# A retention-and-gated-FFN kernel: one load of v issued later on GpSimd, and a gate block put ahead of one transposition

## The chip, the cores and the metric

One Trainium2 chip, one core of it. The metric is the device time of one execution in microseconds (us), median of the runs shown.

## The reference, cut to what matters

```python
def _attn_ref(q, k, v):                     # q, k, v: (4, 8, 768, 64)
    gamma = 1.0 - 2.0 ** (-5.0 - np.arange(H))
    for t in range(S):
        state = gamma * state + einsum('bhd,bhe->bhde', k[:, :, t], v[:, :, t])
        y[:, :, t] = scale * einsum('bhd,bhde->bhe', q[:, :, t], state)

def _moe_ref(x, w_gate, w_val, w_out):      # x: (3072, 512), d_ff = 1536
    gate = 1.0 / (1.0 + np.exp(-(x @ w_gate)))
    val = x @ w_val
    return gate * val @ w_out
```

The output of the first, with heads side by side, is the x of the second. Inputs and output are float32.

## The kernel before, in words

The sequence of 768 is cut into six tiles of 128 positions; the four batch entries go through together, two at a time. A **pair** P is tile P // 2 with batch entries 0 and 1 (P even) or 2 and 3 (P odd), so there are 12 pairs; a pair has two **chunks**, its two batch entries. For each pair k and q are brought to the transposed layout qkT: by TensorE transposes for pairs 0 to 3 (`transpose`, L200, and the eviction `turned_out`, L210), by DMA transposes from SP for pairs 4 to 11 (`xbar`, L219). Then come the scores (`scores`, L238), the masks that take them out of PSUM on VectorE (`mask`, L243), the part of y that comes from the carried state (`inter`, matmuls of zbd and qkT), the part within the tile (`intra`, L258), y's way into xT (`y_out`, L271 or L273), and the state update (`state`, L280, and what follows it). A matmul that `mm` issues is one of 128x128 at L305, or two of 64 columns at L309, by a flag.

For each tile of 512 tokens the FFN then multiplies xT by the gate and value weights (`up`, `up_half`; from tile 1's later part on by a scheme of seven half-size products, which needs sums of weight blocks), applies the sigmoid on ScalarE, the product on VectorE or GpSimd, and the down projection. The sums of weight blocks are `weight_sums` (L456, into wt and scr) and `halves_sums` (L361, into ws, wg, wv); hidden ones are `hidden_sums` (L474).

Nothing is scheduled by a planner when the kernel is built: the order of the work is a written list, `ORDER`, of six strings. Each word is a step with two letters and a number; a capital first letter makes `mm` issue whole matmuls, a small one halves, and + and - say which tile's FFN is meant. Each engine executes its own instructions in this order. The steps that the change and the prediction speak of:

- `in4`, `ia4`, `yo4`: `inter`, `intra`, `y_out` of pair 2, chunk 0; with 5 of pair 2, chunk 1. `mk8` and `mk9` are the two masks of pair 2, chunk 0; `mk10` and `mk11` those of chunk 1.
- `tp6`, `te6`: the TensorE transposes of pair 3's k and their eviction on ScalarE; `tp7`, `te7` those of pair 3's q.
- `vm10`, `vm11`, `mu10`, `mu11`: value blocks of tile 0 on TensorE and their products on VectorE. `ag2`, `ag6`: gate blocks of tile 1 (256 columns, two blocks of hidden units each).
- `sc6`, `sc8`, `sc10`: scores of chunk 0 of pairs 3, 4 and 5. `sm5`, `sm6`: state update of pairs 5 and 6. `xk4`, `xq4`, `xk5`, `xq5`: DMA transposes of pairs 4 and 5.
- `wp..`, `wc..`: weight sums on GpSimd and their copies out on ScalarE. `hg6`: a hidden sum of tile 0 on GpSimd (L474).

Loads of k, q and v and of the weights go out on GpSimd's queue (`load`, L96; L116; L120), in program order and mixed with GpSimd's arithmetic. All loads up to pair 5 stand ahead of the first step of `ORDER`. Buffers rotate by the digits in `PLACES`; ff are the seven PSUM banks.

Of the kernel before, what the change touches and what calls it, by code (L numbers as in the profile page):

```python
# [17 lines left out]
def kernel(  # L18
# [38 lines left out]
        "gs": "01234501234503215034203502345102354130524301453201540321453034035412031524",  # L57
        "maskd": "01",
        "ff": (
            "012345601230465102346523105246310542631405314056321602341562034163412045632516523560132601562306"  # L60
            "251062562015020324512065630653102651604250142343624015405400652016203541034046326504510416035253"
            "245132541351025162405034123406520512341234160532120605410531324"
        ),
        "qkT": "010231230123",
        "kt": "0101100101",
        "st": "012345670123456702134675120346752104637563245710",
        "xT": "010101",
        "hT": "010101",
        "scr": "010101101001101010010101010101",
# [12 lines left out]
    def held_in(P, n):  # L82
        held = {"k": kn, "q": qn, "v": vn}[n]
        t, j = divmod(P, 2)
        if (n, t) not in lands:
            lands[n, t] = place(ld, [C, 4 * H, D], BF16, tag=n, name=n + "n")
        for i in range(2):
            held[2 * t + i] = lands[n, t][:, i * 2 * H:(i + 1) * 2 * H, :]
        return held[P]

    def load(P, *what, pairs=1):
        t, j = divmod(P, 2)
        for n in what:
            held_in(P, n)
            x = {"k": k, "q": q, "v": v}[n]
            nc.gpsimd.dma_start(out=lands[n, t][:, j * 2 * H:(j + pairs) * 2 * H, :],  # L96
                                in_=x[2 * j:2 * (j + pairs), :, t * C:(t + 1) * C, :].rearrange("b h s d -> s (b h) d"))
# [85 lines left out]
    qkT, kt, sc, st, y, zz, za, xT = {}, {}, {}, {}, {}, {}, {}, {}  # L183
# [377 lines left out]
    def hold(P):  # L561
        nc.gpsimd.tensor_copy(kept[:, :2], qkT[P][:, :, 1, NP - 1, C - 1])

    def hold_for_sums(t):
        nc.gpsimd.tensor_copy(kept[:, 2:3], hs[t][:, 2, NFF // 2 - 1, :1])
# [53 lines left out]
    for s in range(4):  # L619
        load_out(s)  # L620
    load(4, "k", "q", "v")
    load(5, "k", "q", "v")

    STEPS = {
        "gm": lambda t, n: up(t, n, 0),
# [38 lines left out]
        "lk": lambda t, P: load(P, "k", pairs=2),  # L664
        "lq": lambda t, P: load(P, "q", pairs=2),
        "lv": lambda t, P: load(P, "v", pairs=2),
        "ho": lambda t, P: hold(P),
        "hi": lambda t, n: hold_for_sums(t),
        "xk": lambda t, P: xbar(P, 0),
# [128 lines left out]
```

## Time and profile before

| | us |
|---|---|
| time, median of 3 runs | 224.1 (215.31 to 226.42) |
| time of the profiled execution | 215.9 |
| its span, first to last instruction | 214.2 |
| TensorE busy | 204.6 (96%) |
| VectorE busy | 189.2 (88%) |
| ScalarE busy | 147.5 (69%) |
| GpSimd busy | 139.5 (65%) |

The shares are averages over stages with different limits. In the rows, PE is TensorE, PEld its weight loads, DVE VectorE, ACT ScalarE, POOL GpSimd, SP the sync engine; a row of the timeline has the start in us, the duration in us, then engine, line, operation, output and input, the number of instructions merged, and in brackets the idle time of the engine ahead of it with what ended it.

### The profile page before, as it was taken

What the parts mean: (1) busy time and instruction counts of PE and PEld (TensorE: products, weight loads), DVE (VectorE), ACT (ScalarE), POOL (GpSimd) and SP (SyncE); (2) the same over time, 40 slices, a digit from 0 to 9 for tenths busy, and PEclk for the clock granted to TensorE, in tenths of its full rate; (3) what the DMA queues carried; (4) which work ended last, traced back from release to release, by engine and by line L of the source; (5) the groups of instructions that cost most, each with busy time, mean ns of one, the idle gap of its engine ahead of it and who ended that gap; (6) DMA issues with size and microseconds to landing.
All of it is one profiled execution on the core that took longest, in us unless ns stands there. A gap on an engine that the chain in (4) does not pass through costs nothing.

```text
span 214.2 us, 7187 instructions
## 1 busy us (share of the span) xinstructions
PE 204.6 (96%) x2938; PEld 177.3 (83%) x2938; DVE 189.2 (88%) x406; ACT 147.5 (69%) x396; POOL 139.5 (65%) x145
## 2 busy tenths in 40 slices
PE   6778999999999999999999999999999999999994
PEld 6555555778888998899988889998899988888883
DVE  6587979989999999979999899999999999968971
ACT  6384466543994389786869798787768969577731
POOL 8977784679999946699764279875618537024500
PEclk9999999999999999999999999999999999999999
DMA  9999999999995999969995129998121000023305
GB/s 125 143 170 194 195 173 165 183 199 159 159 132 33 98 156 143 204 126 157 170 227 115 49 99 163 159 105 127 49 101 52 3 0 3 0 50 70 75 25 183
DMA packets 103922, 25.38 MB, mean 118 GB/s; under 512 B 93904, under 2 KB 101072, under 8 KB 103888
## 3 DMA queue, kind: packets, MB, share of 16 engines
q0 software_dynamic: 81104, 13.90, 84.6%
q1 hardware_dynamic: 22640, 10.88, 28.6%
q8 instruction: 23, 0.38, 0.7%
q10 hardware_dynamic: 144, 0.13, 0.2%
q14 instruction: 11, 0.09, 0.1%
HBM read 28.31 MB, written 6.29 MB: 162 GB/s over the span
## 4 chain that ended last, share of the span: by engine, by line
PE 76%; DMA 14%; POOL 4%; DVE 3%; issue 1%; ACT 0%; ACTq 0%; DVEq 0%; POOLq 0%
PE ff L305 41%; PE ff L309 29%; DMA qn<-in_q_dram 6%; DMA wg<-in_moe_w_gate_dram 4%; DMA vn<-in_v_dram 4%; PE ff L238 2%; PE ff L258 2%; DVE scr L414 1%; POOL kn L96 1%; PE z L280 1%; DVE gs L435 1%; DVE xT L273 1%; POOL vn L96 1%; POOL qn L96 1%; POOL kn L104 1%
## 5 line engine op out<-in xcount | busy, mean ns | idle before, releaser
L420 POOL TENSOR_TENSOR hT<-gs,scr 128x512 bf16<-128x512 f32 x17 | 22.1, 1302 | 21.4 <-ACT gs L440 9.0
L430 ACT COPY gs<-ff 128x256 f32<-128x256 f32 x72 | 25.6, 377 | 11.1 <-PE ff L305 5.7
L409 ACT COPY scr<-ff 128x256 f32<-128x256 f32 x72 | 25.2, 375 | 6.5 <-PE ff L309 3.6
L414 DVE TENSOR_TENSOR scr<-scr,ff 128x512 f32<-128x512 f32 (+1 forms) x48 | 25.6, 547 | 3.5 <-ACT scr L409 1.3
L435 DVE TENSOR_TENSOR gs<-gs,ff 128x512 f32<-128x512 f32 (+1 forms) x48 | 25.8, 548 | 3.2 <-PE ff L305 2.0
L510 ACT COPY ob<-ff 128x256 f32<-128x256 f32 x48 | 17.7, 375 | 15.2 <-PE ff L305 8.9
L243 DVE TENSOR_TENSOR st<-ff,maskd 128x512 bf16<-128x512 f32 x40 | 25.7, 682 | 0.9 <-PE ff L238 0.9
L440 ACT ACTIVATE gs<-gs 128x512 f32<-128x512 f32 (+1 forms) x48 | 24.7, 530 | 2.3 <-DVE gs L435 2.2
L309 PE MATMUL ff<-xT,wg 128*64 128x256 bf16 (+1 forms) x268 | 24.2, 308 | 0.0
L309 PEld LDWEIGHTS <-wg 128*64 128x64 bf16 x356 | 19.4, 110 | 4.1 <-issue 0.4
L423 POOL TENSOR_TENSOR hT<-gs,scr 128x256 bf16<-128x256 f32 x16 | 11.9, 747 | 15.9 <-ACT gs L440 12.0
L309 PE MATMUL ff<-xT,wv 128*64 128x256 bf16 (+1 forms) x220 | 21.5, 311 | 0.0
L305 PEld LDWEIGHTS <-hT 128*128 128x128 bf16 x198 | 19.2, 98 | 2.7 <-issue 0.2
L305 PE MATMUL ff<-wo,hT 128*128 128x256 bf16 x156 | 21.0, 273 | 0.0
L309 PEld LDWEIGHTS <-wv 128*64 128x64 bf16 x312 | 17.2, 110 | 4.2 <-issue 0.3
L305 PEld LDWEIGHTS <-wv 128*128 128x128 bf16 x184 | 17.7, 98 | 2.4
L305 PEld LDWEIGHTS <-wg 128*128 128x128 bf16 x162 | 15.7, 98 | 3.8 <-issue 1.1
L309 PE MATMUL ff<-xs,ws 128*64 128x256 bf16 x208 | 18.7, 273 | 0.0
L305 PE MATMUL ff<-xT,wv 128*128 128x256 bf16 (+1 forms) x134 | 18.5, 276 | 0.0
L231 ACT ACTIVATE kt<-kn,tabk 128x128 bf16<-128x128 bf16 x48 | 18.3, 405 | 0.1
L309 PEld LDWEIGHTS <-ws 128*64 128x64 bf16 x308 | 17.2, 110 | 0.3
L305 PE MATMUL ff<-xT,wg 128*128 128x256 bf16 x110 | 15.4, 272 | 1.6 <-ACT xT L271 1.6
(118 smaller groups left out, 526.8 us busy)
## 6 DMA issues: line engine op xcount, KB each, us to landing
out_dram<-ob SPq DMA_DIRECT2D x18, 256.0 KB, 3.3
vn<-in_v_dram POOLq DMA_DIRECT2D x6, 256.0 KB, 12.4
wo<-in_moe_w_out_dram POOLq DMA_DIRECT2D x4, 384.0 KB, 14.2
kn<-in_k_dram POOLq DMA_DIRECT2D x3, 512.0 KB, 7.8
qn<-in_q_dram POOLq DMA_DIRECT2D x3, 512.0 KB, 10.0
vn<-in_v_dram POOLq DMA_DIRECT2D x3, 512.0 KB, 11.6
out_dram<-ob SPq DMA_DIRECT2D x11, 128.0 KB, 2.2
kn<-in_k_dram POOLq DMA_DIRECT2D x5, 256.0 KB, 13.4
```

What stands on the lines that cost most here:

```text
L231: nc.scalar.activation(to[:, :, h, :], x[:, :, h, :], AX.Copy, scale=tabk[:, 0, h:h + 1])
L243: nc.vector.tensor_tensor(st[P, c, i], sc[P, c][i], (mask0 if P < 2 else maskd)[:, i], op=ALU.mult)
L305: nc.tensor.matmul(o, left, right, skip_group_check=True, **kw)
L309: nc.tensor.matmul(o[half], left[:, half], right, skip_group_check=True, **kw)
L409: nc.scalar.copy(vals[t, g][:, {1: 0, 5: 2, 3: 1}[n]], m[False][:, 256:] if n == 1 else m[True][:, :256])
L414: nc.vector.tensor_tensor(o, o, x, op=ALU.add)
L420: eng.tensor_tensor(h[:, 2 * g], s, vals[t, g][:, 0:2].rearrange("p two n -> p (two n)"), op=ALU.mult)
L423: eng.tensor_tensor(h[:, 2 * g + 1, 256:], s[:, 256:], vals[t, g][:, 2], op=ALU.mult)
L430: nc.scalar.copy(o, pairs[t, g, 0][x][:, :256] if x else pairs[t, g, 0][x][:, 256:])
L435: nc.vector.tensor_tensor(o, o, pairs[t, g, 0][False][:, cols], op=ALU.add)
L440: nc.scalar.activation(o, x, AX.Sigmoid)
L510: nc.scalar.copy(o, fast[t, i][x][:, :256] if x else fast[t, i][x][:, 256:])
```

## The change

The load of pair 5's v leaves the block of loads and becomes a step, `lw5`, behind `hg6`. In the second string of `ORDER` pair 2's chunk 0 moves ahead: its masks go in front of tile 0's last products, `in4` and `ia4` in front of `vm11`, and `in4` is issued in halves. The gate block `ag2` goes between `tp6` and `tp7`. Three more words move by a few places: `dc11`, `dc15` and `hs7` of tile 0, and in the third string `sm6`, which now stands behind `gs57`. The digits of `PLACES` for the banks and for st follow the new order.

```diff
-    load(5, "k", "q", "v")
+    load(5, "k", "q")
...
+        "lw": lambda t, P: load(P, "v"),
...
-        "zo0- wp1 gm7- ... sg10- mu6- mu8- mk10- mk8-  "
-        "mk11- wp8 vm10- mu10- wp2 in5 ia5 vm11- IN4 mk9- ia4 yo5 tp6 yo4 aw13 sg11- te6 mu11- tp7 te7 dd5 dd15  "
-        "ag2 ag6 kt24 xk5- as2 sc6 ...
+        "zo0- wp1 gm7- ... sg10- mu6- mu8- mk10- mk11-  "
+        "mk8- mk9- wp8 vm10- wp2 in5 in4 ia5 ia4 yo5 yo4 vm11- mu10- tp6 aw13 sg11- te6 mu11- ag2 tp7 te7 dd5  "
+        "dd15 ag6 kt24 xk5- as2 sc6 ...
...
-        ... zo6 hg6- BV0 AV0 ...
+        ... zo6 hg6- lw5 BV0 AV0 ...
...
-        ... ia15 gp44 ga56 gs56 va56 vf46 vf56 sm6 vp47 va47 in14 gp57 ga57 gs57 vp57
+        ... ia15 gp44 ga56 gs56 va56 vf46 vf56 vp47 va47 in14 gp57 ga57 gs57 sm6 vp57
```

On GpSimd, at the end of the block of loads and then 14 rows later (kn, qn, vn are the landing tiles of k, q and v; ws, wt, scr and wg belong to the weight sums, hT to `hg6`):

```order
 L96 DMA qn<-in_q_dram 128x16x64
-L96 DMA vn<-in_v_dram 128x16x64
 L361 TENSOR_TENSOR ws<-wv 128x256
 L456 TENSOR_TENSOR wt<-wo 128x512
...
 L361 TENSOR_TENSOR wg<-wg 128x2x128
 L474 TENSOR_TENSOR hT<-hT 128x2x256
+L96 DMA vn<-in_v_dram 128x16x64
 L456 TENSOR_TENSOR wt<-wo,scr 128x512
 L456 TENSOR_TENSOR scr<-wo 128x512
```

The load of v has moved past 14 instructions of arithmetic on GpSimd.

On VectorE, where pair 2's masks (st), its y (xT) and tile 0's last products (hT) stand:

```order
-L243 TENSOR_TENSOR st<-ff,maskd 128x512 x3
-L332 TENSOR_TENSOR hT<-gs,ff 128x512
-L243 TENSOR_TENSOR st<-ff,maskd 128x512
-L273 TENSOR_TENSOR xT<-ff,taby_138 128x4x128 x2
-L332 TENSOR_TENSOR hT<-gs,ff 128x512
+L243 TENSOR_TENSOR st<-ff,maskd 128x512 x4
+L273 TENSOR_TENSOR xT<-ff,taby_138 128x4x128 x2
+L332 TENSOR_TENSOR hT<-gs,ff 128x512 x2
```

The same eight instructions: the fourth mask and the two of y now stand ahead of both products.

More of the change, by code (lines that the diff above doesn't have):

```diff
@@ L59 @@
         "ff": (
-            "012345601230465102346523105246310542631405314056321602341562034163412045632516523560132601562306"
-            "251062562015020324512065630653102651604250142343624015405400652016203541034046326504510416035253"
-            "245132541351025162405034123406520512341234160532120605410531324"
+            "012345601230465102346523105246310542631405314056321632045631205430541256301643610634201432461036"
+            "142361461324313015421364603640231642635143251050615324534533641326130452305356016435423526304140"
+            "154201452042314261534305210536413421052105263401213634523402015"
         ),
@@ L65 @@
         "kt": "0101100101",
-        "st": "012345670123456702134675120346752104637563245710",
+        "st": "012345670123456701234675210346751204637563145720",
         "xT": "010101",
```

14 rows, old and new, of the table ORDER are left out of this document.

## The prediction

> **What bounds the kernel now.** I read the page's shares first, then the busy time by stages, then the chain that ended last, and then the timelines of the four engines around the moved steps. The profiled execution took 215.9 us, 1.7 us more than its span of 214.2; all sums below are made against that execution. It stands near the lowest of the three runs shown (215.31), 8.2 us under their median of 224.1, and no profile of a run at 224 exists.
>
> ```profile
> 41.00:62.00 21.00, 20.98 (x282) 18.39 (x283) 19.87 (x35) 14.42 (x31) 19.04 (x19) 1.00 1.89 170
> 62.00:77.00 15.00, 15.00 (x276) 13.73 (x276) 14.54 (x28) 8.02 (x20) 14.82 (x15) 1.00 1.25 86
> 77.00:111.00 34.00, 33.86 (x601) 31.36 (x596) 32.24 (x76) 26.84 (x81) 24.40 (x26) 1.00 1.69 174
> 111.00:175.00 64.00, 63.98 (x1019) 59.14 (x1017) 60.50 (x130) 52.00 (x150) 39.50 (x37) 1.00 0.72 87
> ```
>
> These rows of the busy time by stages (stage, its length, then busy time of PE, PEld, DVE, ACT, POOL, the granted clock, DMA share, GB/s) say that from 41 us on TensorE has no hole worth the name, at a granted clock of 1.00. So a step that only changes places behind 41 us is worth nothing unless it opens a hole, and a gain can come only from the stretch where TensorE still waits for a load. That stretch is in the chain that ended last:
>
> ```profile
> 27.54 13.44 DMA qn<-in_q_dram
> 41.02 0.64 PE ff L200 x16
> ```
>
> Pair 3's q, issued at 27.54 us, lands at 40.98, and `tp7` starts on it at once. From there the chain is TensorE nearly to the end.
>
> **The early part: the new order around `tp7`.** TensorE and the two engines that feed it, before:
>
> ```profile
> 37.94 0.39 PE L309 MATMUL ff<-qkT,zbd 128*64 128x128 bf16 x8
> 38.16 0.52 PE L258 MATMUL ff<-st,vn 128*64 128x128 bf16 x8
> 38.49 1.05 PE L309 MATMUL ff<-xT,wv 128*64 128x512 bf16 x8
> 39.48 0.40 PE L305 MATMUL ff<-qkT,zbd 128*128 128x128 bf16 x4
> 39.81 0.41 PE L258 MATMUL ff<-st,vn 128*64 128x128 bf16 x8
> 40.05 0.61 PE L200 MATMUL ff<-ident,kn 128*64 128x128 bf16 x16
> 41.02 0.64 PE L200 MATMUL ff<-ident,qn 128*64 128x128 bf16 x16 [0.36 <-DMA qn<-in_q_dram]
> 41.49 1.91 PE L309 MATMUL ff<-xT,wg 128*64 128x256 bf16 x32
> 43.34 0.62 PE L238 MATMUL ff<-qkT 64*128 64x128 bf16 x16
> ```
>
> ```profile
> 36.36 1.89 DVE L243 TENSOR_TENSOR st<-ff,maskd 128x512 bf16<-128x512 f32 x3
> 38.22 0.69 DVE L332 TENSOR_TENSOR hT<-gs,ff 128x512 bf16<-128x512 f32 x1
> 38.82 0.68 DVE L243 TENSOR_TENSOR st<-ff,maskd 128x512 bf16<-128x512 f32 x1
> ```
>
> ```profile
> 40.71 2.01 ACT L210 COPY qkT<-ff 128x1024 bf16<-128x1024 bf16 x2 [2.34 <-PE ff L200]
> ```
>
> Each row is start, duration, engine, line, operation and tiles. They are, from the top, `in5`, `ia5`, `vm11`, `in4` (whole), `ia4`, `tp6`, `tp7`, `ag2` with `ag6`, `sc6`; three masks, `mu10`, the fourth mask; `te6` with `te7`. What one costs is the distance of starts: a halved `in` 0.22 us, the whole one 0.33, an `ia` 0.22 to 0.24, `vm11` 0.87, `tp6` 0.44, `tp7` 0.47, a gate block 0.925 (half of 43.34 - 41.49). The one stall that is named is 0.36 us at `tp7`; the whole `in4` also starts about 0.13 us after `vm11` has had its 0.87.
>
> Now the new order from 37.94. `in5`, `in4` and `ia5` end at 37.94 + 3 x 0.22 = 38.60. `ia4` needs the fourth mask, which has lost `vm11` as its cover: three masks end at 36.36 + 1.89 = 38.25, the fourth starts at 38.22 where `mu10` stood and ends at 38.90; with 0.05 to start, `ia4` runs at 38.95, after **a new stall of 0.35 us**, and ends at about 39.15. `vm11` to 40.02, `tp6` to 40.46. `ag2` needs both parts of y, which VectorE now takes straight after the masks at 0.60 each from 38.85: ready at about 40.15, so `ag2` goes at 40.46 and ends at 41.39. Pair 3's q has been there since 40.98, so `tp7` does not wait: 41.39 to 41.86. `ag6` to 42.78. But `sc6` needs `te7`. A transposition's records last to 0.64 us behind its start and ScalarE follows 0.04 later: `te7` goes at 41.39 + 0.68 = 42.07 and takes half of 2.01, to 43.07. So `sc6` starts at about **43.10 instead of 43.34, a gain of 0.24 us**, with TensorE idle for the 0.32 us ahead of it. Of the 0.36 us of the load, most goes to the fourth mask and to `te7`: what is late next is ScalarE's eviction, since only one gate block now lies behind `tp7` where two did.
>
> Bounds: if neither the mask nor `te7` held TensorE up, the gain would be 0.36 + 0.13 + 0.11 (the halved `in4`) = 0.60 us; if `te7` comes as late as before, nothing. I take the worked 0.24.
>
> **The load of v: GpSimd's side.** The moved load is 1.14 us of GpSimd, with 0.59 us of waiting ahead of it.
>
> ```profile
> 44.68 1.14 POOL L96 DMA_DIRECT2D qn<-in_q_dram  x1 [0.89 <-DMA wo<-in_moe_w_out_dram]
> 46.41 1.14 POOL L96 DMA_DIRECT2D vn<-in_v_dram  x1 [0.59 <-DMA wo<-in_moe_w_out_dram]
> ...
> 54.98 1.16 POOL L456 TENSOR_TENSOR scr<-wo 128x512 f32<-128x512 bf16 x1 [0.25 <-ACT wo L460]
> ...
> 62.06 1.21 POOL L456 TENSOR_TENSOR wt<-wo,scr 128x512 bf16<-128x512 bf16 x1
> ...
> 79.96 1.15 POOL L474 TENSOR_TENSOR hs<-hT,hs 128x512 bf16<-128x512 bf16 x1 [3.10 <-PE ff L309]
> ```
>
> The sums begin at 45.82 instead of 47.56, 1.74 us earlier. That head start dies at 54.98, where a sum waits until ScalarE has copied scr out (L460), and ScalarE gets there in its own order behind the gates of TensorE; it comes only the 0.24 us earlier. So `hg6`, the instruction ahead of 62.06, ends at about 61.8, the load of v is issued from 61.8 to 63.0, and what stands behind it on GpSimd is **0.9 us later than before**. Behind it are a sum that ScalarE copies out at 66.35, pair 6's loads, and xs; the 3.10 us of waiting ahead of 79.96 takes the delay up. ScalarE's copy goes from 66.35 to 67.2, but its next gate waited 0.94 us for TensorE, which covers that:
>
> ```profile
> 66.35 0.62 ACT L460 CAST wt<-scr 128x512 bf16<-128x512 f32 x1 [1.28 <-POOL scr L456]
> 67.91 0.60 ACT L345 ACTIVATE gs<-ff 128x512 f32<-128x512 f32 x1 [0.94 <-PE ff L305]
> ```
>
> I cost it at nothing; with that cover gone it would be up to 0.9 us.
>
> **The load of v: the queue's side.** v is first read by `sm5`, the state update of pair 5.
>
> ```profile
> 64.29 0.62 PE L238 MATMUL ff<-qkT 64*128 64x128 bf16 x16
> 69.02 0.62 PE L238 MATMUL ff<-qkT 64*128 64x128 bf16 x16
> 69.58 0.44 PE L280 MATMUL z<-vn,kt 128*64 128x64 bf16 x16
> ```
>
> The rows are `sc8`, `sc10` and `sm5`, which would come at 69.34. How long 256 KB take from 61.8 no row shows: before, issued at 46.41, the load queued behind everything else for the 17.5 us of the first row below. The page's rows of DMA issues (KB each, median us to landing) bound it. Below: 4.9 us, what 128 KB took at the start. Above: 12.4, the median of v's 256 KB loads. Nearest are the 512 KB loads of k, which go out when the queue has run empty: 7.8. I take 6.4, between 4.9 and 7.8: landing at 68.2, **1.1 us ahead of `sm5`**, so nothing is paid. At 7.8 it is 69.6 and 0.3 us are lost.
>
> ```profile
> DMA to landing us min/median/max: 17.5/17.5/17.5
> ```
>
> ```profile
> vn<-in_v_dram POOLq DMA_DIRECT2D x6, 256.0 KB, 12.4
> kn<-in_k_dram POOLq DMA_DIRECT2D x3, 512.0 KB, 7.8
> kn<-in_k_dram POOLq DMA_DIRECT2D x1, 128.0 KB, 4.9
> ```
>
> In return the load no longer shares the DMA engines with the transposes from SP until 63.9 (46.41 + 17.5). Those of pair 4's q and pair 5's q, the latter issued when that q had landed, and under each its time to landing:
>
> ```profile
> 53.64 3.64 SPq L219 DMA_TRANSPOSE qkT<-qn  x1
> ```
>
> ```profile
> DMA to landing us min/median/max: 10.1/10.1/10.1
> ```
>
> ```profile
> 61.44 1.57 SPq L219 DMA_TRANSPOSE qkT<-qn  x1
> ```
>
> ```profile
> DMA to landing us min/median/max: 5.4/5.4/5.4
> ```
>
> They land at 63.7 and 66.8, 0.5 us ahead of `sc8` and 2.2 ahead of `sc10`. `sc8` did not wait, so there is nothing to gain, only cover.
>
> The Trainium skill, DMA: Bandwidth & Descriptors, section Queues, rings and completion order, says that each DMA engine goes round the queues that have work, packet by packet. By that rule the moved load relieves pair 4's transpose and burdens pair 5's; the sum stays at -0.24 unless the burden passes 2.2 us, and that is the third rival.
>
> The rest costs nothing: `sm6` moves by four short steps, and the other words shift ScalarE copies and a hidden sum, in stages whose TensorE is busy for 33.86 of 34.00 and 15.00 of 15.00 us; no row names a wait that they end.
>
> **Sum**: 215.9 - 0.24 + 0 + 0 = **215.7 us**.
>
> **The rivals.** (1) The wait only changes its name: the fourth mask and `te7` eat the whole 0.36. The worked times leave 0.32 us of idling ahead of `sc6`, which speaks for it. 215.9 us. (2) **Slower**: the load of v is late for `sm5`. It decides once the load takes over 7.5 us from 61.8; at the 12.4 of the page it lands at 74.2 and TensorE, in order, stands 4.9 us: 215.7 + 4.9 = 220.5, 2.1% more. Against it, the 12.4 is from loads with several others in the queue, and the DMA rate falls soon after 64 us (86 GB/s in the stage 62 to 77). (3) Pair 5's transpose of q takes the 10.1 us of pair 4's: it lands at 71.5 and `sc10`, due at 68.8, waits 2.7: 218.4. Against it, pair 4's ran beside three loads, this one beside one. (4) The measurement falls where the median of before lies: loads land later in all, TensorE waits longer at `tp7` and `sc8`. The change then covers up to 0.925 us at the one and 2.5 (from 61.44, when pair 5's q had landed, to 63.9, the moved load's turn in the queue) at the other: 224.1 less 0.2 to 3.4, so 220.7 to 223.9. For it, two of three runs; against, that nothing in the trace says those runs differ by their loads.
>
> **How the numbers follow.** The forecast 0.45, rival 1 0.10, rival 2 0.11, rival 3 0.05, rival 4 0.29. The forecast's own range is 214.8 (the 0.60 of the bounds, and 0.5 of scatter between 215.31 and 215.9) to 216.3; to leave out no more than 2 in 10 the range goes on through rivals 1 to 3 and most of 4: 214.8 to 224.5. Two per cent, 4.3 us, is about what a measurement of this kernel can tell from no change. Forecast and rivals 1 and 3 are within it, set against 215.9. The runs shown lie 11 us apart, and that enters too: 215.7 set against 224.1 reads as 3.7% faster (a third of the forecast's 0.45, and a little of rival 4: 0.18), 220.7 to 223.9 set against 215.9 as 2.2 to 3.7% slower (0.04 of rival 4, with the 0.11 of rival 2: 0.15). Within 2%: 0.67.
>
> **What the profile after would show.** Right: no idle time for the DMA of qn at `tp7`; a stall of about 0.35 us at `ia4` released by VectorE's mask, and one of about 0.3 at `sc6` released by ScalarE's eviction; `sc6` near 43.1; GpSimd waiting some 2 us for ScalarE near 53 to 55; v issued near 62 and no wait of `sm5`. Wrong: a wait of TensorE for vn near 69, for qkT at `sc8` or `sc10`, `sc6` not before 43.3, or any new hole in TensorE behind 70 us.

## The result and the profile after

The changed kernel is slower: 218.2 us, median of 20 executions (216.14 to 224.55), against 216.0 us for the kernel before beside it (20 executions, 215.13 to 226.42). The ratio is 1.0055, interval 1.0031 to 1.0078; it leaves out executions more than 1.5% above the fastest of their kernel. These are part of the story here: over all series of this study 16 of 28 executions of the changed kernel lay above 218 us, and 14 of 140 of the kernel before. The profiled execution took 216.14 us, 0.24 more than that of before, with a span of 214.4 us.

The busy time by stages of the changed kernel (columns as in the prediction):

```profile
41.00:62.00 21.00, 20.77 (x278) 18.15 (x274) 18.14 (x36) 14.45 (x32) 18.04 (x18) 1.00 1.75 168
62.00:77.00 15.00, 14.98 (x276) 13.64 (x275) 14.76 (x27) 7.84 (x20) 14.94 (x15) 1.00 1.20 84
77.00:111.00 34.00, 33.71 (x592) 30.82 (x589) 32.24 (x75) 26.32 (x79) 24.46 (x27) 1.00 1.68 170
```

TensorE has lost busy time in the first stage (20.98 before; the 0.23 us at `sc6`, which the prediction expected), but also in the third (33.86 before), in which nothing was moved but `sm6`. The timeline, from the top: `in5` with `in4`, `ia5` with `ia4`, `tp7`, `sc6`, `sc8`, and two places in the third stage:

```profile
37.80 0.61 PE L309 MATMUL ff<-qkT,zbd 128*64 128x128 bf16 x16
38.25 0.90 PE L258 MATMUL ff<-st,vn 128*64 128x128 bf16 x16
...
41.14 0.64 PE L200 MATMUL ff<-ident,qn 128*64 128x128 bf16 x16
...
42.88 0.62 PE L238 MATMUL ff<-qkT 64*128 64x128 bf16 x16 [0.23 <-ACT qkT L210]
...
63.83 0.81 PE L238 MATMUL ff<-qkT 64*128 64x128 bf16 x16
...
79.25 0.41 PE L309 MATMUL ff<-xT,ws 128*64 128x256 bf16 x4 [0.27 <-DVE ws L361]
...
85.23 0.38 PE L305 MATMUL ff<-xT,ws 128*128 128x256 bf16 x2
```

and the same two places before:

```profile
79.08 0.39 PE L309 MATMUL ff<-xT,ws 128*64 128x256 bf16 x4
...
84.87 0.38 PE L305 MATMUL ff<-xT,ws 128*128 128x256 bf16 x2
```

Followed along TensorE: `tp7` no longer waits, and `sc6` stands at 42.88 instead of 43.34, 0.46 us ahead; 0.14 of it was there already at `in5` (37.80 for 37.94), ahead of what was changed on TensorE. `sc8` is still 0.46 ahead when it starts (63.83 for 64.29) but takes 0.81 for 0.62, 0.19 longer: 0.27 left. At 79.25 the lead has become a lag of 0.17, and at 85.23 one of 0.36. So 0.46 us were won and about 0.8 lost later. What holds the matmul at 85.23 the profile does not name. The loss at 79 us is VectorE beside GpSimd, after and before:

```profile
76.28 1.17 POOL L371 TENSOR_TENSOR xs<-xT 128x512 bf16<-128x512 bf16 x1
...
76.66 1.07 DVE L474 TENSOR_TENSOR hs<-hT 128x512 bf16<-128x512 bf16 x1
```

```profile
75.70 1.17 POOL L371 TENSOR_TENSOR xs<-xT 128x512 bf16<-128x512 bf16 x1
...
76.94 0.42 DVE L474 TENSOR_TENSOR hs<-hT 128x512 bf16<-128x512 bf16 x1
```

GpSimd's xs is 0.58 us later, VectorE's hidden sum 0.28 earlier. Before, the one had ended (76.87) when the other began; now they meet, VectorE's 0.42 us become 1.07, and it ends 0.28 after GpSimd's. The matmul of ws then waits for VectorE: the hole of TensorE behind 70 us that the prediction had named as a sign of being wrong.

The other rows of GpSimd that the prediction rests on:

```profile
44.15 1.14 POOL L96 DMA_DIRECT2D qn<-in_q_dram  x1 [0.56 <-DMA wo<-in_moe_w_out_dram]
45.31 0.68 POOL L361 TENSOR_TENSOR ws<-wv 128x256 bf16<-128x256 bf16 x1
...
54.52 1.39 POOL L456 TENSOR_TENSOR scr<-wo 128x512 f32<-128x512 bf16 x1 [1.90 <-ACT wo L460]
...
61.45 1.19 POOL L96 DMA_DIRECT2D vn<-in_v_dram  x1
```

```profile
DMA to landing us min/median/max: 5.4/5.4/5.4
```

The first weight sum starts at 45.31 instead of 47.56, 2.25 us earlier (worked: 1.74), the head start dies in a wait of 1.90 us for ScalarE, and v lands 5.4 us after its issue, at 66.9, well ahead of `sm5`.

### The profile page after: what moved, and what is told of

It is laid out like the page before. It is cut to its first block, busy times and chain, and to the rows that moved or that the text cites. A ratio compares the mean times of both kernels' runs of the same rounds, so it can differ in the third digit from the quotient of the medians.

```text
span 214.4 us, 7194 instructions
## 1 busy us (share of the span) xinstructions
PE 204.5 (95%) x2942; PEld 177.7 (83%) x2942; DVE 187.9 (88%) x406; ACT 147.5 (69%) x396; POOL 139.4 (65%) x145
## 4 chain that ended last, share of the span: by engine, by line
PE 83%; DVE 12%; ACT 2%; issue 1%; ACTq 0%; DVEq 0%
PE ff L305 42%; PE ff L309 31%; PE ff L238 3%; PE ff L258 2%; DVE st L243 2%; PE ff L537 2%; PE ff L200 2%; DVE xT L273 2%; PE z L280 1%; DVE hT L332 1%; DVE scr L414 1%; DVE hs L474 1%; ACT xT L271 1%; ACT qkT L210 1%; DVE ws L361 1%
```

## Experiments

All are variants of the two kernels, each timed beside the kernel before on the same chip. "Over 218" counts executions; the ratio is as above. The rows come from five series (4, 4, 3, 3 and 2 rows) on four chips; the kernel before beside them was over 218 us in 0 of 11, 2 of 24, 5 of 28, 0 of 29 and 2 of 20, so a share over 218 of one series is only roughly comparable with that of another.

| kernel | median | before beside it | ratio, interval | over 218 |
|---|---|---|---|---|
| order alone | 216.05 | 215.36 | 1.0019, 0.9992 to 1.0045 | 1 of 6 |
| load of v alone | 219.58 | 215.36 | 1.0055, 1.0024 to 1.0086 | 3 of 6 |
| v in the gap | 215.7 | 215.36 | 1.0008, 0.9983 to 1.0033 | 1 of 6 |
| xs first | 217.09 | 215.36 | 1.0059, 1.0017 to 1.0101 | 3 of 6 |
| after again | 219.61 | 215.65 | 1.0032, 1.0018 to 1.0047 | 5 of 8 |
| iota ahead of the sums | 217.2 | 215.65 | 1.0065, 1.0049 to 1.0082 | 0 of 6 |
| one sum earlier | 216.7 | 215.65 | 1.0063, 1.0036 to 1.0089 | 5 of 11 |
| gap, one sum earlier, hs7 | 215.48 | 215.65 | 1.0011, 0.9978 to 1.0043 | 2 of 11 |
| order and hs7 | 215.7 | 215.87 | 0.9997, 0.9977 to 1.0017 | 4 of 12 |
| iota between the sums | 216.78 | 215.87 | 1.0062, 1.0030 to 1.0093 | 2 of 11 |
| before again | 215.72 | 215.87 | 0.9995, 0.9975 to 1.0016 | 0 of 8 |
| both sums early | 216.48 | 215.67 | 1.0065, 1.0030 to 1.0099 | 5 of 12 |
| v in the gap, again | 216.67 | 215.67 | 1.0020, 0.9991 to 1.0050 | 3 of 12 |
| gap, both sums early, hs7 | 215.42 | 215.67 | 0.9984, 0.9970 to 0.9998 | 1 of 11 |
| both sums early, hs7 | 216.8 | 215.64 | 1.0076, 1.0044 to 1.0108 | 1 of 9 |
| gap, both sums early, hs7, again | 215.43 | 215.64 | 1.0001, 0.9981 to 1.0020 | 1 of 12 |

**Order alone**: the new order, v back in the block of loads.

```diff
-    load(5, "k", "q")
+    load(5, "k", "q", "v")
-  ... zo6 hg6- lw5 BV0 ...
+  ... zo6 hg6- BV0 ...
```

> The change without its move of the load of v: v of pair 5 is issued with the block again, all else as changed. Theory A (the loss comes from the load of v, which makes GpSimd 0.6 us late, so that its xs at 76.28 runs beside VectorE's hidden sum at 76.66 and stretches it from 0.42 to 1.07 us): xs is back near 75.3, the hidden sum takes 0.42, TensorE has no hole near 79, and the time is 0.3 to 0.5 us under before. Theory B (the new order itself costs what it gives, by the hidden sum and the copies that it moves): at or above before, like the change.

**Load of v alone**: the kernel before with `lw5` behind `hg6`.

```diff
-    load(5, "k", "q", "v")
+    load(5, "k", "q")
-  ... zo6 hg6- BV0 ...
+  ... zo6 hg6- lw5 BV0 ...
```

> The kernel before with the load of v alone moved behind the sums. Theory A: xs runs near 76.5 beside VectorE's hidden sum, which takes about 1.0 us, TensorE waits 0.3 to 0.6 us near 79 for ws, and nothing is won at the transposition of pair 3's q: 0.5 to 0.9 us over before. Theory B: the load costs nothing, time as before within 0.2 us.

**v in the gap**: the changed kernel with `lw5` where GpSimd waits 1.9 us for ScalarE.

```diff
-  ... ag4 as4 wp5 dd7 ...      ... hg6- lw5 BV0 ...
+  ... ag4 as4 lw5 wp5 dd7 ...  ... hg6- BV0 ...
```

> The change, with the load of v put ahead of the sum for which GpSimd waits 1.90 us for ScalarE (54.52 in the changed kernel). Theory A: GpSimd is not late behind it, the hidden sum near 76.5 takes 0.42, no hole of TensorE near 79: 0.3 to 0.5 us under before, 0.6 to 1.0 under the change. Theory B: as the change within 0.2 us.

**xs first**: the changed kernel with GpSimd's xs ahead of its load of v for pair 6.

```diff
-  ... vc05 lv6- gp15 xg1 ...
+  ... vc05 xg1 lv6- gp15 ...
```

> The change, with GpSimd's xs ahead of its load of v for pairs 6 and 7, so that xs runs about 1.7 us earlier and nothing else on GpSimd reads SBUF while VectorE's hidden sum runs. Theory A: the hidden sum takes 0.42 us, the hole of TensorE near 79 is gone: 0.5 to 0.7 us under the change. If it is GpSimd's lateness as such and not the meeting of the two instructions, the hole stays and the time is that of the change within 0.2 us.

The load is what costs: alone it gives the whole 1.0055. Put into the gap it costs nothing that the ratio shows, and the order alone neither gains nor loses measurably; the 0.3 to 0.5 us under before that were expected of both do not show. The meeting at 76 us is real: with xs at 74.67, 75.06 or 75.51 us (xs first, gap, order alone) the hidden sum takes 0.42 us in each profile and TensorE's wait at 79 is gone. But with xs first the median stays 1.7 us above before and 3 of 6 executions above 218 us, so that meeting is not the whole loss. Another loss was in the profile of the load alone, which fell on an execution of 222.29 us:

```profile
44.70 4.46 DVE L361 TENSOR_TENSOR ws<-wg,ws 128x256 bf16<-128x256 bf16 x1
```

```profile
43.85 1.14 POOL L96 DMA_DIRECT2D qn<-in_q_dram  x1 [0.53 <-DMA wo<-in_moe_w_out_dram]
45.00 0.68 POOL L361 TENSOR_TENSOR ws<-wv 128x256 bf16<-128x256 bf16 x1
45.64 1.16 POOL L456 TENSOR_TENSOR wt<-wo 128x512 bf16<-128x512 bf16 x1
46.75 1.15 POOL L456 TENSOR_TENSOR scr<-wo 128x512 f32<-128x512 bf16 x1
47.86 1.14 POOL L456 TENSOR_TENSOR wt<-wo 128x512 bf16<-128x512 bf16 x1
49.21 1.15 POOL L456 TENSOR_TENSOR wt<-wo 128x512 bf16<-128x512 bf16 x1 [0.21 <-DMA wo<-in_moe_w_out_dram]
```

```profile
50.25 0.44 PE L280 MATMUL z<-vn,kt 128*64 128x64 bf16 x16 [3.23 <-DVE za L290]
```

```profile
46.00:50.00 4.00, 0.97 (x7) 0.60 (x7) 4.00 (x5) 0.25 (x1) 3.79 (x4) 1.00 1.91 177
50.00:54.00 4.00, 3.60 (x42) 2.57 (x42) 4.00 (x10) 1.73 (x3) 2.10 (x3) 0.58 2.48 156
```

A sum of VectorE with both operands in SBUF, elsewhere 0.28 us, lasts 4.46. It ends at 49.16, in the 0.21 us in which GpSimd waits for a DMA after four sums in a row. State updates behind it on VectorE are late, TensorE stands 3.23 us, and in the next stretch its granted clock is 0.58. In the profile of the changed kernel the same sum starts at the same time and is out 0.24 us before GpSimd's first sum, at 45.31:

```profile
44.70 0.37 DVE L361 TENSOR_TENSOR ws<-wg,ws 128x256 bf16<-128x256 bf16 x1
```

Without the load of v behind pair 5's q, GpSimd's sums start about 2.2 us earlier, and VectorE's sum at 44.7 escapes them in one execution and not in the next. That is the theory of the starved sum, which the second round tests. No execution of the changed kernel above 217 us was profiled, so for its own long executions the theory rests on the variants.

**After again**: the changed kernel.

> The changed kernel once more, beside the three below. Theory S (starved sum): with pair 5's v load gone from between its q load and GpSimd's first weight sum, that sum starts about 2.2 us earlier than before (45.3 for 47.6 us) and VectorE's sum of two operands in SBUF (line 361, ws from wg and ws, at 44.7) has a margin of only 0.3 to 0.6 us; where it misses it, GpSimd's sums in a row keep it out for 4 us or more. About half of the executions should lie above 218 us (11 of 20 did), the others at 216.2 to 216.6. Theory T (the spread has nothing to do with the change; it is the chip): this kernel and the kernel before should have the same share of executions above 218 us on this chip, about 1 in 8 each.

**Iota ahead of the sums**: GpSimd writes an unused tile nine times where the load of v was.

```diff
     load(5, "k", "q")
+    idle = const.tile([128, 128], F32, name="idle")
+    for _ in range(9):
+        nc.gpsimd.iota(idle, pattern=[[1, 128]], base=0, channel_multiplier=-1, ...)
```

> The changed kernel, and in place of the v load that went away GpSimd writes an unused tile nine times (iota, 128x128, about 0.19 us each by the row at 0.91 to 1.10 us, 1.7 us in all), which puts its first weight sum back to about 47 us. It adds work and restores nothing of the load. Theory S: executions above 218 us become rare, 1 in 10 or fewer, as before the change, and the undisturbed ones stay at 216.0 to 216.5 us, since the xs sum is then as late as in the changed kernel or later. Theory T, or the theory that the place of the v load behind the sums of tile 0 is what makes executions long: about half stay above 218 us.

**One sum earlier**: `dd7`, VectorE's sum at 44.7, two places ahead.

```diff
-  ... mk12 dd20 sc7 mk15 sm3 ag4 as4 wp5 dd7 ag0 ...
+  ... mk12 dd20 dd7 sc7 mk15 sm3 ag4 as4 wp5 ag0 ...
```

> The changed kernel with one VectorE instruction moved two places ahead: the sum ws from wg and ws (line 361) stands before the mask that it followed, so that it starts at about 44.1 us instead of 44.7, 1.2 us ahead of GpSimd's first weight sum instead of 0.6; that mask ends 0.2 us later. Theory S: executions above 218 us drop from half to 1 in 5 or fewer, undisturbed ones stay within 0.3 us of 216.3. The rival that another sum further on is the one held up (in the long execution on record also one at 66.5 us, 2.0 us): no drop. Theory T: no drop.

**Gap, one sum earlier, hs7**: the last, with v in the gap and `hs7`, `dc11`, `dc15` at their places of before.

> The new order with the three losses taken out: pair 5's v load in GpSimd's idle 1.9 us ahead of its wait for ScalarE, the VectorE sum two places ahead as in the kernel beside it, and the last-tile hidden sum and its two copies (hs7, dc11, dc15) at their places of before. Theory S with the losses read from the traces: 0.46 us gained at pair 3's scores and nothing lost at 64 and 79 us, so 215.0 to 215.4 us for the middle execution, 0 to 0.5 us under the kernel before, and few executions above 218 us. The rival that the order itself costs about as much as it gains: level with before, 215.4 to 215.9 us.

The iota runs, which add 2.71 us to GpSimd, have no execution above 217.5, where the changed kernel beside them has five of eight from 219.5 to 226.5. VectorE's sum runs beside the iotas in its own 0.28 us:

```profile
44.65 0.28 DVE L361 TENSOR_TENSOR ws<-wg,ws 128x256 bf16<-128x256 bf16 x1
```

```profile
44.52 2.71 POOL L625 IOTA idle<- 128x128 f32 x9
47.20 0.67 POOL L361 TENSOR_TENSOR ws<-wv 128x256 bf16<-128x256 bf16 x1
```

So neither the count of GpSimd's instructions nor the late place of v makes those executions long by itself. But the expected return to 216.0 to 216.5 was missed: four of six lie at 217.2 to 217.5, and the one profile (216.26) does not show why. One sum earlier did not help: 5 of 11, where 1 in 5 or fewer was expected. In its profile (221.83 us) GpSimd's first sum is 0.5 us earlier than in the profile of the changed kernel and VectorE's sums 1.5 us later (45.44 for 43.90), as late as TensorE already is at `tp6` (41.36 for 39.82). So two places did not bring them ahead of GpSimd, and both VectorE sums, now adjacent, were caught.

```profile
45.44 2.42 DVE L361 TENSOR_TENSOR ws<-wg 128x256 bf16<-128x256 bf16 x1
47.78 1.26 DVE L361 TENSOR_TENSOR ws<-wg,ws 128x256 bf16<-128x256 bf16 x1
```

```profile
44.80 0.69 POOL L361 TENSOR_TENSOR ws<-wv 128x256 bf16<-128x256 bf16 x1
```

With v in the gap and hs7 back as well, the median is 215.48, not under before as hoped but level with it (1.0011), as its rival said; in its profile (217.3 us) the two sums take 0.74 and 1.24 us.

**Order and hs7**: the order alone, with `hs7`, `dc11` and `dc15` back.

> The new order with pair 5's v load back between its q load and GpSimd's first weight sum, and with the hidden sum of the last tile and its two copies (hs7, dc11, dc15) at their places of before. What is left of the change is pair 2's second chunk and the gate block ahead of pair 3's transposes. Starved-sum theory: the load holds GpSimd's sums back to about 46.6 us, so executions above 218 us are as rare as before (1 in 10); with the meeting at 79 us and the stop at 64 us gone too, the middle execution stands at 215.2 us, about 0.4 us under the kernel before if the wait of 0.44 us ahead of pair 3's transposes of q in the profile of before is there in most of its executions. Rival: that wait is an accident of one profiled execution, and the kernel is level with before within 0.2 us.

**Iota between the sums**: one iota behind each of GpSimd's first four sums.

> The changed kernel with one iota (128x128, 0.3 us in a row by the run with nine of them, 2.71 us) behind each of GpSimd's first four weight sums, none ahead of the first: that sum starts as early as in the changed kernel (45.0 to 45.5 us), so VectorE's sum still meets it as often. Theory S1 (VectorE waits as long as GpSimd has one sum behind the other that reads SBUF, and gets in at the first gap): an iota lets VectorE in, the hold is at most one GpSimd sum, 0.7 to 1.3 us instead of 2.4 to 4.4 us, and executions lie at 216.2 to 218 us, hardly any above 219. Theory S2 (the hold has a length of its own and gaps do not matter): about half stay above 219 us, as in the changed kernel. In the profile, a held sum of VectorE would end where an iota begins.

**Before again.**

> The kernel before, for a second profile of it. If the wait of PE for pair 3's q (0.44 us ahead of its transposes, a DMA that lands late) is there again, the step that the forecast took its gain from is a property of the kernel; if PE goes straight on there, the forecast's gain was read from an accident of one execution, and the execution is then about 0.4 us shorter, at 215.3 to 215.5 us.

Iota between the sums leaves 2 of 11 above 218 and none above 220 (10 of 28 of the changed kernel are), which agrees with gaps letting VectorE in; its profile, 216.78 us, shows no sum caught at 45 us, so the mechanism is not shown there. The second profile of before has no wait for pair 3's q at all (`in5`, `tp7`, `sc6`):

```profile
38.53 0.39 PE L309 MATMUL ff<-qkT,zbd 128*64 128x128 bf16 x8
...
41.10 0.61 PE L200 MATMUL ff<-ident,qn 128*64 128x128 bf16 x16
...
43.48 0.62 PE L238 MATMUL ff<-qkT 64*128 64x128 bf16 x16
```

TensorE came to `in5` 0.59 us later than in the first profile and found q there; the execution took 216.02 us, no shorter. From the start of `in5` to that of `sc6` the old order needs 4.95 us here, 5.26 in the profile of the load alone, with 0.20 us of waiting for q, and 5.40 in the first profile of before, with 0.36. The changed kernel needs 5.08 (42.88 - 37.80), and the order alone and the order with hs7 back the same within 0.01, each with 0.23 us for ScalarE ahead of `sc6`. So the new order is ahead only where the old one waits for q, and 0.13 us behind where q is there in time. The order with hs7 back has a profile 0.7 us shorter in span (213.5), but its median of 215.7 is level with before, as its rival said, and 4 of its 12 executions lie at 222.8 to 226.9, where 5 of 28 of the kernel before beside it lie at 223 to 229. What makes these long no profile here caught; that stays open.

**Both sums early**: `dd7` and `dd20` ahead of the scaling of pair 3's k, GpSimd untouched.

```diff
-  ... dd15 ag6 kt24 xk5- as2 sc6 mk12 dd20 sc7 mk15 sm3 ag4 as4 wp5 dd7 ag0 ...
+  ... dd15 ag6 dd7 dd20 kt24 xk5- as2 sc6 mk12 sc7 mk15 sm3 ag4 as4 wp5 ag0 ...
```

> The changed kernel with both of VectorE's weight sums (line 361, at 43.9 and 44.7 us) ahead of the scaling of pair 3's k, where they start at about 41.5 us, 3.5 us ahead of GpSimd's first weight sum; VectorE's idle 0.59 us ahead of the mask at 43.3 pays for them. GpSimd's work is untouched, its sums start as early as in the changed kernel. Starved-sum theory: no VectorE sum of two SBUF operands stands between 43 and 50 us, so executions above 218 us fall from about half (16 of 28) to 1 in 6 or fewer, and the others stay at 216.2 to 216.6 us. Rival, that GpSimd's early sums or the late load of v make executions long in another way: about half stay above 218.

**v in the gap, again.**

> The changed kernel with pair 5's v load in GpSimd's idle 1.9 us, once more: its GpSimd sums start as early as in the changed kernel (45.35 us), yet only 1 of 6 executions was above 218 us. If the early sums alone make an execution long, about half of these lie above 218 us. If the load of v behind the sums for tile 0 is needed too (it sets GpSimd back again at 61 us, beside VectorE's next sums), 1 in 5 or fewer do.

**Gap, both sums early, hs7.**

> The new order with the load of v in GpSimd's idle 1.9 us, the two VectorE sums ahead of the scaling of k, and the hidden sum of the last tile with its two copies at their places of before. By the traces 0.5 us gained at pair 3's scores and nothing given back: the undisturbed executions at 214.9 to 215.3 us, the middle one under 215.4, 0.3 us or more under the kernel before, and executions above 218 us in 1 of 6 or fewer. Rival, that the order is worth nothing: 215.5 to 215.8, level with before.

**Both sums early, hs7**: v stays behind `hg6`.

> The changed kernel with VectorE's two weight sums ahead of the scaling of k, and the last tile's hidden sum hs7 with its two copies at the places of before; pair 5's v load stays behind GpSimd's sum hg6 at 61 us. Against the kernel with only the first of these edits, of whose executions 5 of 12 lay at 218.2 to 219.5 us and whose profile showed VectorE held at 59.5 to 64.5 us and PE stopped 1.66 us. If the early place of hs7 is the cause of that second hold, 1 in 8 or fewer stay above 218 us. If it is the load of v issued at 61 us, which sets GpSimd's sums behind it against VectorE's in another phase, 4 in 10 stay there. The undisturbed ones at 216.0 to 216.4 us in both cases, since the xs sum is still late.

**Gap, both sums early, hs7, again.**

> The new order with v in GpSimd's idle 1.9 us, the two weight sums ahead of the scaling of k and hs7 back, once more on another chip. If its gain of 0.25 us in the middle execution (ratio 0.9984) and its narrow spread (10 of 11 within 215.1 to 215.5 us) are its own, the ratio lies again between 0.997 and 1.000 and nine in ten executions lie within 0.6 us; if they came with that chip, it is level with before and as spread out.

Both sums early took away what lay above 220 us (0 of 12, against 10 of 28 of the changed kernel in other series), but 5 of 12 stayed at 218.2 to 219.5, where 1 in 6 or fewer were expected above 218. That fits a first meeting that gives the longest executions, and a second. The last two kernels show it in the same phase, one with the load of v behind `hg6` and one without. With it (217.83 us):

```profile
60.79 1.31 DVE L474 TENSOR_TENSOR hs<-hT,hs 128x512 bf16<-128x512 bf16 x1
62.03 2.36 DVE L361 TENSOR_TENSOR ws<-ws,wg 128x256 bf16<-128x256 bf16 x1
```

```profile
60.68 1.15 POOL L474 TENSOR_TENSOR hT<-hT 128x512 bf16<-128x512 bf16 x1
61.77 1.19 POOL L96 DMA_DIRECT2D vn<-in_v_dram  x1
62.98 1.18 POOL L456 TENSOR_TENSOR wt<-wo,scr 128x512 bf16<-128x512 bf16 x1
```

```profile
65.75 0.61 PE L305 MATMUL ff<-wo,hs 128*128 128x256 bf16 x4 [1.55 <-DVE hs L474]
```

Without it (216.78 us):

```profile
60.79 1.42 DVE L474 TENSOR_TENSOR hs<-hT,hs 128x512 bf16<-128x512 bf16 x1
62.13 1.25 DVE L361 TENSOR_TENSOR ws<-ws,wg 128x256 bf16<-128x256 bf16 x1
```

```profile
60.77 1.15 POOL L474 TENSOR_TENSOR hT<-hT 128x512 bf16<-128x512 bf16 x1
61.89 1.34 POOL L456 TENSOR_TENSOR wt<-wo,scr 128x512 bf16<-128x512 bf16 x1
```

```profile
64.73 0.61 PE L305 MATMUL ff<-wo,hs 128*128 128x256 bf16 x4 [0.54 <-DVE hs L474]
```

The two kernels differ only in the place of that load. Its issue, 1.19 us between two GpSimd sums, keeps VectorE's sum out for 1.11 us more, and TensorE's wait grows by 1.01, about the 1.05 us between the two executions. With v behind `hg6` but `hs7` back, 1 of 9 lies above 218, which by the expectation speaks for the early place of `hs7` as the cause of the second hold; but three more lie at 217.6 to 217.9, the ratio is no better, and the profile shows the hold at work with `hs7` at its old place. How much each of the two has in it stays open. With v in the gap alone 3 of 12 stay above 218 (4 of 18 with the first series), and in its profile the two sums at 44 to 45 us take 0.43 and 0.64 us: the early sums still meet VectorE there. With both sums early, v in the gap and `hs7` back most of the spread goes: 18 of 23 executions lie from 215.0 to 215.5 us, two above 218 (226.9 and 226.8). That version has ratios of 0.9984 (0.9970 to 0.9998) and, on another chip, 1.0001 (0.9981 to 1.0020), where 0.997 to 1.000 again and nine in ten executions within 0.6 us were expected (it was 8 of 12). It is level with before; a gain is not shown.

## Why the prediction was wrong

- **The early part was right for the one execution it was read from.** The load's wait went, a short stop for ScalarE came ahead of `sc6` (0.23 us, worked 0.32), and from `in5` to `sc6` 0.32 us were saved (worked 0.24). No row names a stall at `ia4`, for which 0.35 was worked (the working took 0.22 for `ia5`, whose rows give 0.33). That this 0.24 would shorten the execution was not borne out: the order alone measures 1.0019 and, with hs7 back, 0.9997. The wait for q that it is taken from was 0.36 us there, 0.20 and nothing in the other two profiles of the old order. So rival 1, no gain, came nearest for the order, but it does not explain a slower kernel.
- **The queue's side was right**: v landed 5.4 us after the issue (taken: 6.4), and `sm5` did not wait. Rivals 2 and 3 did not happen in the after profile: pair 4's transposition of q took 8.1 us for 10.1, as forecast, and pair 5's 4.2 for 5.4, where a burden was forecast. Nor did rival 4, which took runs near 224 us for the usual ones: the median of before is 216.0 over 20 executions.
- **The step that failed is GpSimd's side: "I cost it at nothing"**. The moved load alone measures 1.0055, as much as the whole change. The working asked who waits for GpSimd's results, found 1.9 and 3.10 us of waiting as cover, and stopped. It did not ask what runs beside GpSimd's moved instructions. Its head start of "1.74 us earlier" was dismissed because it dies at the wait for ScalarE; on the way it can put four sums in a row against VectorE's sum at 44.7, which in the profile of the load alone cost 4.46 us of VectorE and 3.23 of TensorE. Its lateness behind v was dismissed because a later wait covers it; on the way it put xs onto a hidden sum (about 0.45 us of TensorE, in the after profile) and the issue itself between VectorE's sums at 61 (1.0 us of TensorE in the pair of profiles above).
- **"The rest costs nothing"** failed for `hs7` and its two copies: with `hs7` ahead of `bm4`, `sc8` takes 0.81 us in the after profile and 0.90 in that of the order alone; in that of the order with hs7 back it takes 0.62, as before. The profile of both sums early names the wait, 0.22 us for VectorE's product (L349). It was the smallest loss.

The hint stood in the profile of before. The same form of one instruction has two durations there:

```profile
44.38 0.28 DVE L361 TENSOR_TENSOR ws<-wg 128x256 bf16<-128x256 bf16 x1
...
61.01 1.24 DVE L361 TENSOR_TENSOR ws<-ws,wg 128x256 bf16<-128x256 bf16 x1
```

```profile
60.77 1.34 POOL L474 TENSOR_TENSOR hT<-hT 128x512 bf16<-128x512 bf16 x1
```

A sum of 256 columns in 0.28 us, and in 1.24 us while GpSimd runs a sum that ends 0.14 us before it. The Trainium skill, SBUF — State Buffer, section Who interferes with whom, states the rule: a VectorE instruction with two inputs in SBUF contends with a GpSimd instruction that reads SBUF, not with one that only writes it. The traces agree on both halves: 1.07 us beside xs for 0.42 without, and 0.28 beside nine iotas. The section also says that the order of issue decides who blocks. The sum of 4.46 us does not bear that out by the starts of the rows: VectorE's is 0.30 us ahead of GpSimd's first sum, and still stood out for four of them.

## What to carry to other kernels

When a step moves off one engine's queue, list what then runs beside each instruction that shifts, not only who waits for it; for GpSimd sums that means every VectorE instruction with two SBUF operands within the shift. In a trace, look for one form of instruction with two durations: the longer one names the neighbour that holds it. Where two engines start from independent waits, a margin of a few tenths of a microsecond in one profile is a coin toss over many executions, so one profile without a meeting does not say that there is none. The same holds for a gain: a wait for a load that one profile shows, here 0.36 us, may be half of that or nothing in the next.

## What the runs showed of the hardware

VectorE's hold need not end with the GpSimd instruction that it met. It lasted 4.46 us through four sums, and ended in GpSimd's first gap, of 0.21 us; but in the pair at 62 us it ended between two GpSimd sums without a gap, and lasted through a DMA issue that stood ahead. What decides which boundary lets VectorE in stays open.

The hold can begin ahead of GpSimd's sum, beside the load that is issued just before it. In seven profiles (after, after again, v in the gap twice, xs first, iota between the sums, and the gap with one sum earlier) a weight sum follows the issue of pair 5's q at once. There the VectorE sum that starts 0.18 to 0.58 us behind the start of this issue takes 0.34 to 0.74 us for its 0.28, and in all seven it ends 0.91 or 0.92 us behind it, before GpSimd's sum begins. Where the load of v or an iota follows instead, the sum takes 0.28 us (order alone, 0.47 us behind the start of the issue; iota ahead of the sums, 0.48). The two that start 0.84 and 0.85 us behind it, 0.3 us ahead of GpSimd's sum, came behind that moment and took 1.24 (gap, one sum earlier, hs7) and 4.46 us (the load alone). What divides them lies between 0.58 and 0.84 us.

A stop of TensorE costs more than itself in some executions. Both sums early had one of 1.66 us in its profile, with one of 0.22 behind it, and then a granted clock of 0.57 for the next stretch, while the kernel with a stop of 1.55 us (both sums early, hs7) kept 1.00 (stages of the first, then of the second):

```profile
63.00:66.00 3.00, 1.20 (x20) 0.81 (x20) 3.00 (x5) 0.74 (x3) 3.00 (x3) 1.00 1.58 131
66.00:70.00 4.00, 4.00 (x32) 3.12 (x26) 2.76 (x6) 0.62 (x1) 4.00 (x6) 0.57 0.00 0
```

```profile
63.00:66.00 3.00, 1.45 (x14) 1.06 (x13) 3.00 (x4) 1.33 (x4) 3.00 (x3) 1.00 1.41 89
66.00:69.00 3.00, 3.00 (x44) 2.51 (x42) 2.94 (x6) 1.29 (x3) 3.00 (x4) 1.00 0.02 1
```

The Trainium skill, TensorE: Matmul & The Clock Gate, section The HAM clock gate, gives half clock after an idle window of about 3.4 us, in windows that run freely of the kernel. Free-running windows would explain that two like stops end differently, but no run here shows the windows; and the low clock came here behind a stop of about half such a window.
